# Query features of two tiles computed in 32-row by 64-column pieces of TensorE, in a fused attention and feed-forward kernel

## The chip, the cores and the metric

One core of a Trainium2 chip runs the kernel. The metric is the device time of one execution in microseconds (us). Before the change the median of three runs is 238.67 us (238.15 to 242.1).

## What is computed

Four sequences of 1088 positions with 4 heads of 32 go through a linear attention whose features are products of two small projections; the result, 4352 tokens of 128, goes through a feed-forward network with 2048 hidden units. Cut from the reference:

```
def phi(x):                                   # S1, S2: 8 x 32
    a = np.einsum('rd,bhsd->bhsr', S1, x)
    b = np.einsum('rd,bhsd->bhsr', S2, x)
    return np.einsum('bhsi,bhsj->bhsij', a, b).reshape(*x.shape[:-1], 64)
q_p, k_p = phi(q), phi(k)
kv = np.einsum('bhsf,bhsd->bhfd', k_p, v);  z = np.sum(k_p, axis=2)
num = np.einsum('bhsf,bhfd->bhsd', q_p, kv)
den = np.einsum('bhsf,bhf->bhs', q_p, z)[..., None] + 1e-06
x = (num / den) laid out as (4352, 128)
out = (s * np.maximum(x @ w_in, 0) ** 2 + b) @ w_out
```

## The kernel before

Tokens are cut into nine tiles, tile 0 of 256 columns and tiles 1 to 8 of 512 (`TILES`, L26), always with features or channels on the 128 partitions. Data types are float32; the two big matrix products of the feed-forward part are made of three products of split operands (high and low halves, `wih`, `wil`, `woh`, `wol`, `xh`, `xl`, `uh`, `ul`), all on TensorE.

The names in the code: `kvphase(b)` makes the key features of a sequence and sums them against the values into `kv` (L193). For a query tile, the two projections have to be spread from 8 + 8 rows a head to 64 products a head, which fill 128 partitions in two groups g. There are two ways to do it. Tile 0 uses `first_features` (L280): the weights `srep` already hold every projection row repeated eight times, so four products with all 128 rows give both factors in PSUM tile `hp`; ScalarE copies one factor to `br` (L291) and VectorE multiplies (L293) into `pq`. All other tiles use `qfeatures` (L336): four small products give the bare projections (L343), a copy takes them to `abq`, and SyncE's queue writes them to DRAM (`qa` twice 32 KB, `qb` four times 128 KB) and reads them back repeated (`pq` and `br`, 512 KB each, L363 and L365); VectorE multiplies (L367). `qattend(t)` then makes numerators and denominators; for tile 1 it is `direct_attend` (L371), which divides without DRAM, and for tiles 2 to 8 the denominators go by DRAM: `dc`, `num`, `rd` and four `rr` transfers (L427 to L444). `ffn(t, jp)` is a pair of 128 hidden units: products into `hp`, relu and square on ScalarE (L483, L485), a split into `uh` and `ul` (L146, L493), products into `ops`.

PSUM has two buffers each of `hp` (two banks), `ops` and `psa`. Every engine runs its instructions in program order. The program order is written out by hand: `ORDER` (L34) is a list of tokens, and each token runs one generator to its next yield. `z` is a dummy product that fills TensorE (L589); `Lk0`, `Lq1`, `Lv0`, `Lw0`, `Ls` issue loads; `k0`, `q1`, `n1`, `p`, `f`, `w0` are steps of the key phase of a sequence, features and attention of a tile, features and attention of tile 0, and the split of a block of weights; `31` is a step of the pair 1 of tile 3. `ON_DVE` (L37) says which copies VectorE makes and not ScalarE. All DMAs are issued by SyncE in this order too.

Of the kernel before, what the change touches and what calls it, by code (L numbers as in the profile page):

```python
# [24 lines left out]
NMAX = 512  # L25
# [33 lines left out]
def attn_ffn_kernel(ctx: ExitStack, tc: tile.TileContext, qT, kT, vp, s64, cst, w_in, w_out, outT):  # L59
    nc = tc.nc  # L60
    PSUM = bass.MemoryType.PSUM
    const = ctx.enter_context(tc.tile_pool(name="const", bufs=1))
    p1 = ctx.enter_context(tc.tile_pool(name="p1", bufs=1))
# [4 lines left out]
    ps_h = ctx.enter_context(tc.tile_pool(name="ps_h", bufs=2, space=PSUM))  # L68
# [6 lines left out]
    tiles = plan_tiles()  # L75
# [4 lines left out]
    qT_t, w_raw, k_in, v_in = {}, {}, {}, {}  # L80
# [176 lines left out]
    qfeat, xhl, x_first = {}, {}, []  # L257
# [8 lines left out]
        xhl[t] = (xh, xl)  # L266
        yield

    srep = const.tile([P, 2, 2, P], F32, name="srep")

    def first_weights():
        for g in range(2):
            w = sk[:, 32 * g:32 * g + 32].rearrange("p (j w i) -> p w j i", j=2, w=2)
            nc.scalar.copy(out=srep[:, 1, g].rearrange("p (j i x) -> p j i x", i=R, j=2),
                           in_=w[:, 1].unsqueeze(2).broadcast_to([P, 2, R, R]))
            nc.vector.tensor_copy(out=srep[:, 0, g].rearrange("p (j i x) -> p j i x", i=R, j=2),
                                  in_=w[:, 0].unsqueeze(3).broadcast_to([P, 2, R, R]))
        yield

    def first_features(t):  # L280
        N = tiles[t][1] - tiles[t][0]
        pq = p1.tile([P, 2, NMAX], F32, name="pq")
        br = p1.tile([P, 2, NMAX], F32, name="br")
        ab = ps_h.tile([P, 2, 512], F32, name="hp")
        for w in (1, 0):
            for g in range(2):
                nc.tensor.matmul(ab[:, w, g * N:(g + 1) * N], srep[:, w, g], qT_t[t][:, :N],
                                 start=(g == 0), stop=(g == 1), skip_group_check=True)
        yield
        ab = ab[:, :, :2 * N].rearrange("p w (a n) -> p w a n", a=2)  # L290
        nc.scalar.copy(out=br[:, :, :N], in_=ab[:, 1])  # L291
        yield
        nc.vector.tensor_tensor(out=pq[:, :, :N], in0=ab[:, 0], in1=br[:, :, :N], op=ALU.mult)  # L293
        qfeat[t] = pq
        yield
# [295 lines left out]

    with tc.manual_schedule():
        gens = {"z": keep_warm(), "Ls": load_s(), "s": s_phase(), "Lcst": load_constants(),
                "sr": first_weights(), "p": first_features(0), "f": first_attend(0)}
        for b in range(B):
            gens[f"Lk{b}"], gens[f"Lv{b}"], gens[f"k{b}"] = load_k(b), load_v(b), kvphase(b)
        for i, x in enumerate(pieces):
            gens[f"Lw{i}"], gens[f"w{i}"] = load_weights(*x), split_weights(*x)
        for t in range(NT):
            gens[f"Lq{t}"], gens[f"q{t}"], gens[f"n{t}"] = load_q(t), qfeatures(t), qattend(t)  # L600
            for jp in range(NPAIR):
                gens[f"{t}{jp}"] = ffn(t, jp) if t else first_ffn(jp)
        for c in ORDER.split():
            next(gens[c], None)
# [47 lines left out]
```

## Time and profile before

| | before |
|---|---|
| median of three runs | 238.67 us (238.15 to 242.1) |
| the profiled execution, its own time | 239.63 us |
| its span | 237.9 us |
| TensorE busy | 229.4 us |
| ScalarE busy | 189.5 us |
| VectorE busy | 176.2 us |
| DMA | 29.84 MB |

The span runs from the first to the last instruction that the profiler recorded; 1.73 us of the run's time lie around it. TensorE's matmuls are pipelined, so durations of neighbours overlap, and the pace of a group is read from the start of one row to the start of the next. An f32 matmul is listed twice (x8 for four instructions).

### The profile page before, as it was taken

The page shows a single profiled execution, that of the slowest core. Times are in us where ns is not written, and L with a number is a line of the kernel's source. Part 1 is how long each engine was busy: PE and PEld are TensorE (multiplying, and loading weights), DVE is VectorE, ACT ScalarE, POOL GpSimd, SP SyncE. Part 2 cuts the span into 40 slices and gives each one's busy share as a digit, 9 for nine tenths or more (in the row PEclk, how much of TensorE's full clock was granted, in tenths as well). Part 3 has the DMA queues.
Part 4 walks back from the last instruction along what each step waited for, and adds up shares of the span by engine and source line. Part 5 has one row for each costly group of instructions (what it writes and reads, how often), then busy time and mean ns, then how long its engine had stood idle before and what let it go on. Part 6 is the DMA issues. An engine that isn't in the chain of part 4 may idle for free.

```text
span 237.9 us, 4007 instructions
## 1 busy us (share of the span) xinstructions
PE 229.4 (96%) x1507; PEld 178.1 (75%) x1508; DVE 176.2 (74%) x236; ACT 189.5 (80%) x238; POOL 2.3 (1%) x15
## 2 busy tenths in 40 slices
PE   8898799899999999999999999999999999999994
PEld 2666568677787876888878768868888888888783
DVE  1789699799987696586965678877758657566783
ACT  3258489698699987779886999697897979897971
POOL 3000000000000000000000000000000000000000
PEclk9999999999999999999999999999999999999999
DMA  6999999578782721472044157201200201000101
GB/s 174 291 388 363 312 294 286 190 204 239 168 235 94 231 55 29 120 193 96 4 118 148 52 106 210 69 3 41 73 0 0 90 0 47 0 0 0 45 4 44
DMA packets 18332, 29.84 MB, mean 125 GB/s; under 512 B 4296, under 2 KB 10440, under 8 KB 18312
## 3 DMA queue, kind: packets, MB, share of 16 engines
q1 hardware_dynamic: 18312, 29.57, 42.1%
q8 instruction: 12, 0.20, 0.3%
q14 instruction: 8, 0.07, 0.1%
HBM read 21.59 MB, written 7.00 MB: 120 GB/s over the span
## 4 chain that ended last, share of the span: by engine, by line
PE 80%; DMA 14%; SPq 2%; ACT 1%; DVE 1%; issue 0%; DVEq 0%
PE ops L499 38%; PE hp L499 36%; DMA qt<-qT 3%; PE psa L416 3%; DMA br<-qb 3%; DMA raw<-w_in 3%; DMA vt<-vp 3%; DMA qb<-abq 2%; PE psa L343 1%; PE psa L224 1%; PE psa L499 1%; ACT w L127 1%; SPq L86 1%; PE psa L202 1%; DVE pq L367 1%
## 5 line engine op out<-in xcount | busy, mean ns | idle before, releaser
L493 DVE TENSOR_TENSOR ul<-u,uh 128x1024 fp32r<-128x1024 f32 (+1 forms) x69 | 81.3, 1183 | 10.4 <-ACT uh L146 9.2
L483 ACT ACTIVATE u<-hp 128x1024 f32<-128x1024 f32 (+1 forms) x72 | 70.2, 976 | 20.7 <-PE hp L499 10.7
L485 ACT ACTIVATE u<-u 128x1024 f32<-128x1024 f32 (+1 forms) x72 | 72.2, 1012 | 1.5
L499 PE MATMUL hp<-xh,wil 128*128 128x512 f32 (+1 forms) x140 | 54.7, 390 | 0.0
L499 PE MATMUL hp<-xl,wih 128*128 128x512 f32 (+1 forms) x140 | 53.3, 381 | 0.0
L499 PE MATMUL hp<-xh,wih 128*128 128x512 f32 (+1 forms) x140 | 53.3, 381 | 0.0
L146 DVE CAST uh<-u 128x1024 fp32r<-128x1024 f32 x45 | 30.9, 689 | 30.0 <-ACT u L485 27.7
L499 PE MATMUL ops<-uh,wol 128*128 128x512 f32 (+1 forms) x136 | 52.2, 384 | 0.0
L499 PE MATMUL ops<-ul,woh 128*128 128x512 f32 (+1 forms) x136 | 51.9, 382 | 0.0
L499 PE MATMUL ops<-uh,woh 128*128 128x512 f32 (+1 forms) x136 | 51.9, 381 | 0.0
L499 PEld LDWEIGHTS hp<-xh,wil 128*128 128x128 f32 x140 | 26.3, 188 | 9.8 <-issue 4.0
L499 PEld LDWEIGHTS ops<-uh,wol 128*128 128x128 f32 x136 | 25.5, 188 | 6.3 <-issue 1.2
L499 PEld LDWEIGHTS hp<-xh,wih 128*128 128x128 f32 x140 | 26.3, 188 | 5.1
L499 PEld LDWEIGHTS hp<-xl,wih 128*128 128x128 f32 x140 | 26.3, 188 | 4.8 <-DVE xl L265 0.2
L499 PEld LDWEIGHTS ops<-ul,woh 128*128 128x128 f32 x136 | 25.6, 188 | 5.2 <-DVE ul L493 0.2
L499 PEld LDWEIGHTS ops<-uh,woh 128*128 128x128 f32 x136 | 25.5, 188 | 4.9
L146 ACT CAST uh<-u 128x1024 fp32r<-128x1024 f32 (+1 forms) x24 | 23.0, 958 | 0.5
L367 DVE TENSOR_TENSOR pq<-pq,br 128x1024 f32<-128x1024 f32 x8 | 9.6, 1206 | 3.3 <-DMA br<-qb 3.3
L210 DVE TENSOR_TENSOR ph<-ab 128x768 f32<-128x768 f32 (+2 forms) x9 | 11.0, 1218 | 0.1
L224 PEld LDWEIGHTS psa<-ph,vt 128*33 128x33 f32 x288 | 8.2, 111 | 1.4 <-issue 1.0
L224 PE MATMUL psa<-ph,vt 128*33 128x64 f32 x288 | 8.8, 220 | 0.0
L577 ACT ACTIVATE ot<-ops,bias,cst_sb 128x512 f32<-128x512 f32 (+1 forms) x9 | 6.7, 745 | 2.7 <-PE ops L499 2.6
(91 smaller groups left out, 145.4 us busy)
## 6 DMA issues: line engine op xcount, KB each, us to landing
qb<-abq SPq DMA_DIRECT2D x32, 128.0 KB
pq<-qa SPq DMA_DIRECT2D x8, 512.0 KB
br<-qb SPq DMA_DIRECT2D x8, 512.0 KB
qt<-qT SPq DMA_DIRECT2D x8, 256.0 KB
raw<-w_in SPq DMA_DIRECT2D x4, 512.0 KB
raw<-w_out SPq DMA_DIRECT2D x4, 512.0 KB
rr<-rd SPq DMA_DIRECT2D x28, 64.0 KB
outT<-ot SPq DMA_DIRECT2D x7, 256.0 KB
```

The source lines that it names most:

```text
L86: nc.sync.dma_start(out=kt[:, c * P:(c + n) * P], in_=kT[:, b * SP + c * P:b * SP + (c + n) * P])
L127: nc.scalar.activation(out=out, in_=high.bitcast(F32), func=AF.Abs, scale=2.0 ** -112)
L146: (nc.vector.tensor_copy if key in ON_DVE else nc.scalar.copy)(out=out, in_=in_)
L210: nc.vector.tensor_tensor(out=ph[:, H * c0:H * (c0 + n)], in0=ab[:, :, 0].unsqueeze(3).broadcast_to([P, H * n, R, R]), in1=ab[:, :, 1].uns ...
L224: nc.tensor.matmul(kvp[64 * g:64 * g + VW, 64 * j:64 * j + 64], v_in[b][:, c0 + c, 2 * j + g], ph[:, H * c0 + 2 * (g * n + c) + j].rearran ...
L367: nc.vector.tensor_tensor(out=pq[:, :, :N], in0=pq[:, :, :N], in1=br[:, :, :N], op=ALU.mult)
L416: nc.tensor.matmul(ps[j][64 * g:64 * g + n, e0:e1], kv_st[b][64 * j:64 * j + 64, g, :n], pq[64 * j:64 * j + 64, g, e0:e1], start=True, sto ...
L483: nc.scalar.activation(out=u[:, :, :N], in_=hp[:, :, :N], func=AF.Relu)
L485: nc.scalar.activation(out=u[:, :, :N], in_=u[:, :, :N], func=AF.Square)
L493: nc.vector.tensor_tensor(out=ul[:, :, :N], in0=u[:, :, :N], in1=f32(uh[:, :, :N]), op=ALU.subtract)
L499: nc.tensor.matmul(out, w, x, start=(first and k == 0), stop=(last and k == len(terms) - 1), skip_group_check=True)
L577: nc.scalar.activation(out=ot[:, s], in_=o[:, :N], func=AF.Identity, scale=s_col, bias=bias)
```

## The change

`first_features` becomes `wide_features`, and tile 1 uses it too (`WIDE`). The weights `srep` now hold for each head its 32 input rows and 64 repeated columns; `s_raw` grows from 128 to 160 columns to carry them. For each factor w, pair j and group g one product takes the 32 rows of head 2j+g and writes 64 partitions (those of j) of PSUM bank g, so eight products of 256 columns do 256 tokens: one such step for tile 0, two for tile 1, each followed by a copy on ScalarE and a multiplication on VectorE. Tile 1's small products, its copy `abq`, its eight DMAs and its multiplication of 1024 columns go. `ORDER` and `ON_DVE` are new throughout.

```
-ORDER = """z z z Lq1 z z z Ls s sr s Lk0 Lcst Lk0 Lk0 Lv0 Lq0 Lw0 z z z z z z Lv0 Lv0 q1 q1 s k0 k0
+ORDER = """z z z z z z z z z z Lk0 Ls z s sr Lk0 Lq0 Lq1 Lk0 Lv0 Lv0 Lw0 Lv0 z z Lcst Lk1 s s k0 k0
...
+WIDE = (1,)
...
-    s_raw = const.tile([P, 128], I32, name="s_raw")
+    s_raw = const.tile([P, 160], I32, name="s_raw")
...
-    srep = const.tile([P, 2, 2, P], F32, name="srep")
+    srep = const.tile([P, 2, R, R], F32, name="srep")
     def first_weights():
...
+        w = sk_all[:, 64:].rearrange("p (w i) -> p w i", w=2)
+        nc.scalar.copy(out=srep[:, 1], in_=w[:, 1].unsqueeze(1).broadcast_to([P, R, R]))
+        nc.vector.tensor_copy(out=srep[:, 0], in_=w[:, 0].unsqueeze(2).broadcast_to([P, R, R]))
+        yield
+
+    def wide_features(t):
+        n = tiles[t][1] - tiles[t][0]
+        M = 256
+        if t == 0:
+            pq = const.tile([P, 2, M], F32, name="pq0")
+            br = const.tile([P, 2, M], F32, name="br0")
+        else:
+            pq = p1.tile([P, 2, NMAX], F32, name="pq")
+            br = p1.tile([P, 2, NMAX], F32, name="br")
+        for c in range(0, n, M):
+            s = slice(c, c + M)
+            ab = ps_h.tile([P, 2, 512], F32, name="hp")
+            for w in (1, 0):
+                for j in range(2):
+                    for g in range(2):
+                        r = slice(D * (2 * j + g), D * (2 * j + g) + D)
+                        nc.tensor.matmul(ab[64 * j:64 * j + 64, g, w * M:w * M + M],
+                                         srep[r, w].rearrange("p i x -> p (i x)"), qT_t[t][r, s],
+                                         start=True, stop=True, skip_group_check=True,
+                                         tile_position=(D * (2 * j + g), 64 * j))
+            yield
+            nc.scalar.copy(out=br[:, :, s], in_=ab[:, :, M:])
+            yield
+            nc.vector.tensor_tensor(out=pq[:, :, s], in0=ab[:, :, :M], in1=br[:, :, s], op=ALU.mult)
+            qfeat[t] = pq
+            yield
...
-                "sr": first_weights(), "p": first_features(0), "f": first_attend(0)}
+                "sr": first_weights(), "p": wide_features(0), "f": first_attend(0)}
...
-            gens[f"Lq{t}"], gens[f"q{t}"], gens[f"n{t}"] = load_q(t), qfeatures(t), qattend(t)
+            gens[f"Lq{t}"], gens[f"q{t}"], gens[f"n{t}"] = load_q(t), (wide_features if t in WIDE else qfeatures)(t), qattend(t)
...
-    s64 = s64.reshape(P, 64)
+    s64 = np.concatenate([s64.reshape(P, 64), np.tile(np.concatenate([S1.T, S2.T], 1), (H, 1))], 1)
```

Where the new order moves instructions is shown at three places. First TensorE's program behind the dummies at its start, before the change (L343 are tile 1's small products, L202 the key projections, L287 tile 0's wide products, L224 the products of key features and values):

```order
L343 MATMUL psa<-qt,sq 32x256 x4
L202 MATMUL psa<-kt,sk 32x96 x24
L287 MATMUL hp<-qt,srep 128x256 x4
L224 MATMUL psa<-ph,vt 33x64 x36
L589 LDWEIGHTS const-bfloat16-1.0
L589 MATMUL ops<-const-bfloat16-1.0 128x512
```

and the same place of the change (its L204, L297, L226 and L237 are the key projections, the new products, the value products and the transposition of the sums):

```order
L204 MATMUL psa<-kt,sk 32x96 x16
L297 MATMUL hp<-qt,srep 64x256 x8
L204 MATMUL psa<-kt,sk 32x96 x8
L297 MATMUL hp<-qt,srep 64x256 x8
L226 MATMUL psa<-ph,vt 33x64 x36
L297 MATMUL hp<-qt,srep 64x256 x8
L237 MATMUL psa<-cst_sb,kvt_96 128x97
L600 LDWEIGHTS const-bfloat16-1.0
L600 MATMUL ops<-const-bfloat16-1.0 128x512
L204 MATMUL psa<-kt,sk 32x160 x8
```

The key projections have become the first real work, tile 1's features lie around the value products, and one dummy stands behind the transposition where before three stood ahead of it and one behind. Ahead of these rows stand 12 dummies before and 13 after.

Second, SyncE's list of DMAs from the first block of weights on, before:

```order
L111 DMA raw_147<-w_in 128x1024
L95 DMA vt<-vp 128x396 x2
L111 DMA raw_257<-w_in 128x1024
L102 DMA qt<-qT 128x512
L354 DMA qa<-abq 32x256
L358 DMA qb<-abq 16x8x256 x2
L86 DMA kt<-kT 128x640
L86 DMA kt<-kT 128x512
L111 DMA raw_295<-w_in 128x1024
L111 DMA raw_297<-w_out 128x1024
L354 DMA qa<-abq 32x256
L358 DMA qb<-abq 16x8x256
```

and after:

```order
L112 DMA raw_148<-w_in 128x1024
L96 DMA vt<-vp 128x396
L121 DMA cst_sb<-cst 128x160
L87 DMA kt<-kT 128x640
L103 DMA qt<-qT 128x512 x2
L87 DMA kt<-kT 128x512
L112 DMA raw_311<-w_in 128x1024
L112 DMA raw_313<-w_out 128x1024
L96 DMA vt<-vp 128x660
L96 DMA vt<-vp 128x528
L87 DMA kt<-kT 128x640
L87 DMA kt<-kT 128x512
```

Tile 1's round trip (`qa`, `qb`, later `pq` and `br`) is gone, and the loads for the second and third sequence and for tiles 2 and 3 (`kt`, `vt`, `qt`) have moved up into its place.

Third, TensorE's program where tile 2's attention begins (L416 before, L427 after), before:

```order
L499 MATMUL hp<-xh,wil 128x512
L499 MATMUL hp<-xl,wih 128x512
L499 MATMUL hp<-xh,wih 128x512
L416 MATMUL psa<-pq,kv_86 64x320 x2
L416 MATMUL psa<-pq,kv_86 33x320 x2
L416 MATMUL psa<-pq,kv_88 64x192 x2
L416 MATMUL psa<-pq,kv_88 33x192 x2
```

and after:

```order
L510 MATMUL ops<-ul,woh 128x258
L510 MATMUL ops<-uh,woh 128x258
L510 MATMUL ops<-uh,wol 128x258
L510 MATMUL ops<-ul,woh 128x258
L510 MATMUL ops<-uh,woh 128x258
L427 MATMUL psa<-pq,kv_86 64x320 x2
L427 MATMUL psa<-pq,kv_86 33x320 x2
L427 MATMUL psa<-pq,kv_88 64x192 x2
L427 MATMUL psa<-pq,kv_88 33x192 x2
```

Twelve products of 258 columns (tile 0's second matrix) now stand ahead of tile 2's attention; before, they stood between it and the first feed-forward product of tile 2. All else between these two points is the same in number: 66 products of 512 columns, 12 of 256, 12 of 258 (24 before) and the same small ones. Over the whole program TensorE has 16 dummies before and 14 after.

## Rows read from the trace of the kernel before

**Rows 1.** The page's busy times, and the share of the 16 DMA engines in 40 slices (tenths).

```profile
span 237.9 us, 4007 instructions
PE 229.4 (96%) x1507; PEld 178.1 (75%) x1508; DVE 176.2 (74%) x236; ACT 189.5 (80%) x238; POOL 2.3 (1%) x15
...
DMA  6999999578782721472044157201200201000101
```

**Rows 2.** The busy time of each engine in two stretches (length, then busy us and instructions of PE, PEld, DVE, ACT and POOL, the granted clock, the DMA share and GB/s).

```profile
0.00:45.40 45.40, 40.18 (x512) 27.48 (x513) 34.05 (x61) 27.87 (x60) 2.27 (x15) 1.00 0.92 300
45.40:234.70 189.30, 189.20 (x1000) 150.65 (x996) 141.76 (x176) 161.67 (x178) 0.00 (x0) 1.00 0.31 84
```

**Rows 3.** Whom TensorE waited for up to 45.4 us (us in total, times, longest).

```profile
PE psa L343 <- DMA qt<-qT: 1.2, 1, 1.2
PE psa L202 <- DMA kt<-kT: 1.1, 2, 0.8
PE psa L416 <- DVE pq L367: 0.8, 1, 0.8
PE ops L589 <- PEq L644: 0.8, 1, 0.8
PE hp L287 <- DMA qt<-qT: 0.8, 1, 0.8
PE psa L202 <- ACT abq L146: 0.2, 1, 0.2
PE ops L589 <- issue: 0.2, 1, 0.2
PE psa L252 <- DVE pq L367: 0.2, 1, 0.2
```

**Rows 4.** TensorE's timeline at the start (start us, us, what, and in brackets the idle time before it and its releaser).

```profile
0.77 5.28 PE L589 MATMUL ops<-const-bfloat16-1.0 128*128 128x512 bf16 x12 [0.77 <-PEq L644]
5.98 0.64 PE L343 MATMUL psa<-qt,sq 128*32 128x256 f32 x8
6.43 0.51 PE L202 MATMUL psa<-kt,sk 128*32 128x96 f32 x16
7.11 0.88 PE L202 MATMUL psa<-kt,sk 128*32 128x96 f32 x32 [0.16 <-ACT abq L146]
8.74 2.00 PE L287 MATMUL hp<-qt,srep 128*128 128x256 f32 x8 [0.75 <-DMA qt<-qT]
10.67 2.21 PE L224 MATMUL psa<-ph,vt 128*33 128x64 f32 x72
13.03 0.60 PE L589 MATMUL ops<-const-bfloat16-1.0 128*128 128x512 bf16 x2 [0.16 <-issue]
```

**Rows 5.** TensorE's timeline at tile 2's attention and at tile 3's; the four products of 512 columns in the second take the array in quarters of 64 by 64.

```profile
44.38 1.08 PE L416 MATMUL psa<-pq,kv 64*64 64x320 f32 x16 [0.84 <-DVE pq L367]
...
58.02 1.08 PE L416 MATMUL psa<-pq,kv 64*64 64x512 f32 x8
59.03 0.50 PE L499 MATMUL ops<-uh,wol 128*128 128x512 f32 x1
```

**Rows 6.** The chain of work that ended last, in order of time, up to 45 us (start us, us, what).

```profile
5.45 6.00 DMA vt<-vp
...
36.11 6.81 DMA br<-qb
...
43.01 1.24 DVE pq L367
```

**Rows 7.** DMA issues of the whole program by tile (count, KB each).

```profile
qb<-abq SPq DMA_DIRECT2D x32, 128.0 KB
pq<-qa SPq DMA_DIRECT2D x8, 512.0 KB
br<-qb SPq DMA_DIRECT2D x8, 512.0 KB
...
qa<-abq SPq DMA_DIRECT2D x16, 32.0 KB
```

**Rows 8.** VectorE's timeline: tile 0's multiplication and tile 1's.

```profile
11.39 0.69 DVE L293 TENSOR_TENSOR pq<-hp,br 128x512 f32<-128x512 f32 x1 [0.43 <-ACT br L291]
...
28.81 1.23 DVE L367 TENSOR_TENSOR pq<-pq,br 128x1024 f32<-128x1024 f32 x1 [0.59 <-DMA br<-qb]
```

**Rows 9.** ScalarE's timeline: the copy of tile 1's small products and the copy of one factor of tile 0.

```profile
6.68 0.37 ACT L146 COPY abq<-psa 128x256 f32<-128x256 f32 x1 [1.60 <-PE psa L343]
...
10.77 0.59 ACT L291 COPY br<-hp 128x512 f32<-128x512 f32 x1 [3.72 <-PE hp L287]
```

**Rows 10.** VectorE's timeline: the last step of tile 2's attention.

```profile
68.31 0.69 DVE L265 TENSOR_TENSOR xl<-rr,xh 128x512 fp32r<-128x512 f32 x1
```

**Rows 11.** TensorE's timeline: two neighbouring products of 258 columns, and the first feed-forward product of tile 2 that needs that last step.

```profile
66.87 0.28 PE L499 MATMUL ops<-ul,woh 128*128 128x258 f32 x1
66.99 0.28 PE L499 MATMUL ops<-uh,woh 128*128 128x258 f32 x1
...
69.08 0.48 PE L499 MATMUL hp<-xl,wih 128*128 128x512 f32 x1
```

**Rows 12.** SyncE's timeline: the first and the last transfers of tile 2's attention.

```profile
46.13 1.31 SPq L427 DMA_DIRECT2D dc<-num  x2
...
61.88 1.44 SPq L444 DMA_DIRECT2D rr<-rd  x3
```

More of the change, by code (lines that the diff above doesn't have):

```diff
@@ new lines @@
+ORDER = """z z z z z z z z z z Lk0 Ls z s sr Lk0 Lq0 Lq1 Lk0 Lv0 Lv0 Lw0 Lv0 z z Lcst Lk1 s s k0 k0 k0 k0 k0 k0 p k0 k0 k0 q1 p q1 p q1 w0 w0 k0 k0 k0 Lq2 Lq3 Lk1 w0 w0 q1 k0 k0 k0 z k1 k0 q1 k0 w0 q1 f n1 Lw2 Lw1 Lv1 Lv1 w0 f k1 f f n1 q2 f q2 f Lk2 Lk2 Lw4 q2 Lw3 q2 Lq4 q2 k1 k1 k1 f f n1 q3 00 01 k1 w2 f w2 n1 w2 k1 k1 w1 w1 q3 00 01 00 k1 k1 n1 w1 w2 k2 w1 w2 01 w4 w4 w3 f k2 w2 k2 k2 Lv2 Lv2 q2 Lw5 q2 q2 Lw6 q2 Lq5 q2 q3 q3 Lk3 q3 Lw7 Lk3 q3 q3 q3 00 n1 01 03 02 w4 n1 k2 w4 k2 q4 k2 k2 w1 w3 03 02 03 02 03 w5 q4 w4 w4 w3 03 w3 04 05 k1 02 04 04 04 05 w5 n1 w3 n1 w3 04 10 11 03 05 10 05 k2 k2 w5 w5 k1 w5 w5 05 q2 w6 w6 10 11 11 12 04 05 n2 n2 10 10 12 12 12 n2 w1 11 11 12 w6 w6 15 q5 k3 13 w7 13 13 15 15 q5 n2 n2 q3 n2 q3 n2 10 12 11 n2 w6 n2 w6 13 13 06 15 15 06 06 q3 06 14 14 w7 13 k3 w7 14 06 14 07 15 q4 n2 Lq7 q4 n2 n3 07 07 n3 n3 w7 k3 w7 07 14 w7 07 17 16 k2 k2 k3 q7 06 07 14 16 16 17 17 Lv3 n2 q5 q5 n2 n2 n2 q4 q4 n3 q4 n3 q4 q4 q4 k3 n2 n2 n2 n3 q5 q7 n3 n3 n3 24 16 16 17 17 24 24 07 20 20 q4 24 24 16 17 23 20 20 20 22 n4 n4 23 23 23 23 k3 n4 22 20 24 21 n3 q7 q5 q5 q7 Lq8 q7 Lv3 n3 n3 07 n4 Lq6 n3 n3 q5 n4 q7 q5 n4 n3 n4 q5 q7 23 k3 k3 q6 26 21 21 22 22 k3 22 21 17 26 26 26 25 22 n4 21 k3 21 27 n3 q6 25 n4 q5 25 25 n3 26 n3 n5 25 27 27 27 n5 31 26 n5 27 31 31 25 30 30 30 34 k3 q8 27 32 q6 q6 q6 n4 n4 q7 n4 q6 n5 q6 q6 n5 n4 n5 q6 n5 n4 n4 17 q6 31 31 30 30 34 34 32 34 34 30 31 33 32 32 n5 27 35 n4 32 33 33 n5 32 34 36 35 35 33 33 35 k3 35 q6 36 q8 n4 n4 36 36 33 37 37 37 37 36 35 40 n6 42 40 37 40 40 40 42 42 n6 44 36 44 44 n6 n5 n5 n5 n5 n5 27 q7 q7 n6 n6 n6 42 42 n5 q8 q8 q8 n6 43 37 41 40 42 37 41 44 44 43 41 43 43 n6 q7 n5 n6 41 41 45 46 44 43 45 41 n7 n5 n5 47 43 45 45 46 46 45 47 n7 50 47 46 46 47 n7 50 50 52 45 50 47 50 52 52 46 53 47 54 50 53 53 n6 n6 n6 q8 q8 n6 q8 q8 n7 n7 n6 n7 n6 n7 52 52 q8 37 53 53 n7 n7 54 54 54 54 n6 51 56 52 51 51 53 55 51 51 56 56 47 55 55 q8 56 56 n6 n6 57 54 51 60 56 n8 55 55 57 57 57 n8 57 61 60 60 61 61 60 60 55 62 62 61 61 63 63 63 62 n7 47 n7 n7 n7 n7 57 64 65 60 61 62 62 63 62 n8 64 64 n8 63 n7 n8 n7 n8 n8 64 64 n8 65 65 66 63 67 64 65 65 66 n7 66 57 67 67 65 n7 70 71 66 66 66 67 67 70 70 70 n8 70 71 71 57 n8 n8 n8 n8 n8 n8 72 73 67 72 71 71 72 72 72 70 74 73 73 74 74 75 71 72 73 73 74 74 75 67 67 75 n8 75 76 n8 73 74 n8 80 75 76 76 76 76 77 75 80 80 77 77 77 80 80 77 81 76 82 81 81 82 83 77 80 81 81 84 83 82 82 82 83 84 84 85 81 83 83 86 82 84 84 85 85 77 86 86 87 83 84 85 85 86 86 85 86 87 87 77 86 87 87 87 87 87 87 87 87"""
@@ L35 @@
 SPLIT_0 = (tuple(range(2, 8)), (3,4,5,6,7))
 DIRECT = (1,)
-ON_DVE = """a7 a8 k21 k31 n21 n30 n31 n50 n51 n60 n61 n81 u10 u11 u12 u14 u15 u21 u23 u26 u27 u30 u31 u33 u34 u35 u36 u40 u41 u42 u45 u47 u50 u51 u52 u53 u55 u56 u57 u60 u62 u63 u64 u65 u66 u71 u72 u74 u75 u77 u81 u82 u83 u84 u85 u86 u87 w0 w5 w6 w7 x0 x1 x2 x3 x5 x6 x8""".split()
+WIDE = (1,)
+ON_DVE = """k21 k31 n21 n40 n51 n60 n61 n80 t1 t3 u06 u10 u11 u13 u14 u16 u17 u21 u24 u27 u31 u33 u34 u35 u36 u40 u41 u42 u44 u46 u47 u50 u51 u52 u53 u54 u55 u56 u60 u61 u62 u63 u64 u66 u67 u70 u71 u73 u74 u75 u80 u81 u82 u83 u84 u85 u86 u87 w3 w4 w5 w6 x1 x2 x3 x4 x5 x6 x8""".split()
@@ L152, in attn_ffn_kernel @@
     ident = cst_sb[:, CID:CID + P]
-    sk = const.tile([P, 64], F32, name="sk")
+    sk_all = const.tile([P, 80], F32, name="sk")
+    sk = sk_all[:, :64]
     sq = const.tile([P, 64], F32, name="sq")
@@ L160, in s_phase @@
         low, high = words(s_raw)
-        mag = const.tile([P, 64], F32, name="sc_m")
+        mag = const.tile([P, 80], F32, name="sc_m")
         magnitude(mag, high)
-        bits = const.tile([P, 64], I32, name="sc_b")
+        bits = const.tile([P, 80], I32, name="sc_b")
         low_bits(bits, low)
         join(bits, mag, bits)
-        with_sign(sk.bitcast(I32), high, bits)
+        with_sign(sk_all.bitcast(I32), high, bits)
         yield
@@ L267, in split_x @@
         yield
-    srep = const.tile([P, 2, 2, P], F32, name="srep")
+    srep = const.tile([P, 2, R, R], F32, name="srep")
     def first_weights():
[L272 to L277, printed above, removed]
-        yield
@@ L280, in first_features @@
[L280 to L295, printed above, removed]
+        w = sk_all[:, 64:].rearrange("p (w i) -> p w i", w=2)
```

1 line of the change is left out of this document (removed).

## Prediction

> **What bounds the kernel now.** The page comes first: TensorE is busy 96% of the span, ScalarE 80%, VectorE 74% [rows 1]. So I ask where TensorE is not busy, and cut the span where the DMA row of the 40 slices drops from nines [rows 1]. From 45.40 to 234.70 us TensorE idles 0.10 us in 189.30; up to 45.40 it is busy 40.18, so it idles 5.22 [rows 2]. In between nothing can be gained by earlier data, and each microsecond of TensorE's work counts. In the first 45.40 us both count: the work and the idle time. The kernel ends when that first stretch ends plus a fixed 189 us plus a tail of 3.2 us (237.9 less 234.70).
>
> Next, who causes the 5.22 us: 0.77 is the start of the program [rows 4], the other 4.45 are mostly data. Loads of queries and keys make 1.2 + 1.1 + 0.8, the wait of tile 2's attention for its multiplication 0.8 [rows 3], and that multiplication itself waits for `br`, which comes back from DRAM at 42.9 (36.11 + 6.81) [rows 6]. The 16 DMA engines are busy 0.92 of this stretch at 300 GB/s [rows 2]. So the first stretch is a queue of bytes, and TensorE is partly filled with dummies there: 12 at the start, 0.43 us apart (5.98 less 0.77, over 12), and four later at 0.3 [rows 4].
>
> **The change, part by part.**
>
> TensorE's work that goes: tile 0's four full products, 10.67 - 8.74 = 1.93 us, or 0.48 each; tile 1's four small ones, 6.43 - 5.98 = 0.45; of the dummies three later ones (0.9) less one more at the start (0.43), so 0.47 [rows 4]. Together 2.85.
>
> TensorE's work that comes: three steps of eight products, 32 rows by 64 columns of the array, 256 columns long. No row shows this form. If the four row pieces ran one after another, each product at the 0.48 of rows 4, a step would take 3.86 us; if all four ran at once and nothing else were paid, 0.96. The nearest row is tile 3's attention: four products of 512 columns in quarters of 64 by 64, 59.03 - 58.02 = 1.01 us [rows 5]. There too different input rows go into the same columns of the array, each of the four pieces streams 512 columns, as in a step here, and they do run at once, since one after another they would take four times 0.96. I take 1.01, so 3.03 for three. Nothing below 0.96 is to be had, because every row piece must stream its 512 columns. The net is 3.03 - 2.85 = +0.18 us of TensorE's work. By itself the wide form is no gain.
>
> One rule of the Trainium skill speaks against the 1.01: "TensorEngine Tiling (Array Packing)", Restrictions and Gotchas, PSUM Pressure, says that different row tiles cannot access one PSUM bank at the same time; here heads 0 and 2 (rows 0 and 64) both write bank 0 of `hp`, and heads 1 and 3 bank 1, though other partitions. The products of rows 5 write a bank of their own for each half of the rows, so no trace here tests it; by the rule at most two would run at once, which is the rival "in pairs" below.
>
> DMA: tile 1's round trip goes: 2 x 32 + 4 x 128 + 512 + 512 = 1600 KB, eight issues [rows 7]. At 300 GB/s [rows 2] that is 5.4 us of the queue. In SyncE's order all else ahead of tile 2's `br` is the same set of loads, 16 KB of `s_raw` apart, so `br` should land near 42.9 - 5.4 = 37.5, and tile 2's product be free at 37.5 + 1.24 + 0.14 = 38.9 (that multiplication and the gap behind it, 43.01 to 44.38 [rows 5, 6]). TensorE, with no wait at all, would be there at 44.38 - 4.45 + 0.18 + 1.44 = 41.6; the 1.44 are the twelve products of 258 columns that now stand ahead of it, 0.12 each (66.99 - 66.87) [rows 11]. So that wait goes with 2.7 us to spare, and the waits for `kt` and `qt` with it, since those loads stand earlier in the queue and on less traffic.
>
> ScalarE and VectorE: for tile 1 a copy of 0.37 and a multiplication of 1.23 become two copies of 0.59 and two multiplications of 0.69: +0.81 and +0.15 us [rows 8, 9]. They are busy 27.87 and 34.05 of 45.40 [rows 2], so this lies in their idle time; without that cover it would cost 0.96.
>
> What TensorE will still wait for, I follow along the new order. After 13 dummies (0.77 + 5.6 = 6.4) come three groups of key projections (0.44 each), two steps at 1.01 and two thirds of the value products (2.2 us for all) [rows 4]: it asks for the last third of sequence 0's values at 11.2. They landed at 11.45 [rows 6] and stand at much the same depth of the queue: 0.3 us. Then small products of `f`, `n1`, `q2` and `q3` follow each other through two `psa` buffers, each to be emptied by ScalarE or VectorE first; I count four such hand-overs at 0.2, as the short waits of rows 3: 0.8. Then the first feed-forward products of tile 1 need `xl`, which VectorE makes behind two blocks of weights: a guess of one such VectorE step, 0.7. Together 1.8 left of 4.45; the bounds are 0 and all 4.45.
>
> Tile 2's chain: in the trace its attention begins at 44.38 and its last step ends at 69.00 [rows 5, 10]; TensorE wants it at 69.08 and is held up a little (0.48 for a product that else takes 0.39) [rows 11]. This chain has no slack. Twelve products leave the stretch, so TensorE now comes 1.44 us sooner after the start of the chain. But SyncE's list from the first `dc` to the last `rr` of tile 2 shrinks from 25 DMAs to 18; it took 46.13 to 63.32, 0.69 each [rows 12], so about 4.8 us are there to shorten the chain. I take 0; the other bound is 1.44 and more.
>
> **The sum.** -4.45 + 1.8 + 0.18 = -2.5 us. Own time 239.63, span 237.9: the span becomes 235.4 and that run 237.1. The median of the runs shown, 238.67, lies 0.96 under the profiled run; 238.67 - 2.5 = **236.2 us**. With idle time between 0 and 3.3 left, 234.4 to 237.7.
>
> **The rivals.**
>
> - *In pairs*: two row pieces at a time, a step 1.93, +0.92 for each of three: 236.2 + 2.8 = 239.0, no change. For it: the new form puts two row pieces on one bank; against it: rows 5.
> - *One after another*: a step 3.86, +8.6 in all: 244.8, slower by over 2%. It lies in the three L297 groups, all before 15 us, and decides from about 3.4 us a step (243.4 - 236.2 over three, plus 1.01); at 1.84 a step the gain is gone. Against it: the quarters of rows 5 run at once.
> - *Tile 2 late*: the chain keeps its 24.6 us, TensorE stops 1.4 us, up to 2.5 with ScalarE's copies in SyncE's way: 237.6 to 238.7. For it: rows 10 and 11 show no slack. Against it: seven DMAs fewer.
> - *Other waits take over*: with the bytes gone, ScalarE and VectorE, which feed the small products, hold TensorE for as long as DMA did: 238.9. For it: VectorE is busy 34.05 of 45.40 [rows 2]; against it: a quarter of its time is still free.
>
> **How the numbers follow.** Forecast 0.60 (234.4 to 237.7), tile 2 late 0.14, in pairs 0.11, other waits 0.08, one after another 0.05, something better 0.02. The range 234.4 to 239.6 takes in all but the last two and the far end of the pairs. About 2% is what a measurement of this kernel can tell from no change: 233.9 and 243.4. To be faster than that, 4.77 us would have to go, and the idle time holds 4.45: 0.02. Slower: one after another, and a little for a stall in the new order that I have not seen: 0.06. Within 2%: 0.92.
>
> **What would show it.** L297 groups of 1.0 us each (right), 1.9 or 3.9 (wrong). DMA waits of TensorE up to 45 us under 0.5 in all, idle time without the start under 2.5, and `br` of tile 2 landed before TensorE asks for it. The long stretch starting 2 to 3 us earlier and still idling under 0.5. I am wrong if TensorE waits at tile 2's first feed-forward product for L267, or if new waits for VectorE or ScalarE before 40 us sum to over 3.

## The result, and the profile of the changed kernel

The changed kernel takes 241.46 us (median of 4 runs, 241.42 to 242.43), the kernel before, beside it, 238.77 us (4 runs, 238.15 to 242.1): a ratio of 1.013 [1.009, 1.017]. It is slower by 1.3%, where 236.2 us had been forecast, and lies above the range of 234.4 to 239.6. The profiled execution has 241.45 us, with a span of 239.7; before it was 239.63 and 237.9, so the two profiles show 1.8 of the 2.7 us.

The page of the changed kernel comes first, as in [rows 1]:

```profile
span 239.7 us, 4059 instructions
PE 233.4 (97%) x1537; PEld 178.6 (74%) x1538; DVE 176.7 (74%) x237; ACT 189.4 (79%) x237; POOL 2.2 (1%) x15
...
DMA  6999896088566654660264065011000110100011
```

TensorE is now idle for 239.7 - 233.4 = 6.3 us, where it was 8.5. So 2.2 us of idle time went, as hoped. But TensorE is busy for 4.0 us more, and the forecast gave it 0.18 of added work. The next view says where: the busy times of each engine in the stretch up to 45.40 us and in the one behind it (columns as in [rows 2]; the second is 191.0 us long here, and was 189.3).

```profile
0.00:45.40 45.40, 42.42 (x557) 29.55 (x559) 35.62 (x64) 30.47 (x63) 2.25 (x15) 1.00 0.83 271
45.40:236.40 191.00, 190.96 (x982) 149.00 (x980) 140.56 (x173) 158.94 (x175) 0.00 (x0) 1.00 0.31 82
```

Up to 45.40 TensorE does 557 matmuls, where it did 512, and idles 2.98 us instead of 5.22. Behind it, it takes 190.96 us for 982 matmuls, where 1000 took 189.20. So the stretch that nothing was to touch has become slower, without any idle time in it. What TensorE still waits for, in the whole span, are two rows (columns as in [rows 3]):

```profile
PE ops L510 <- DVE wol L485: 1.8, 1, 1.8
PE ops L600 <- PEq L656: 0.8, 1, 0.8
```

All waits for DMA are gone; 0.8 is the start of the program (it was there before), and one wait of 1.8 us is new. TensorE's timeline around the places of [rows 4, 5] (columns as there):

```profile
0.77 5.61 PE L600 MATMUL ops<-const-bfloat16-1.0 128*128 128x512 bf16 x13 [0.77 <-PEq L656]
6.32 0.87 PE L204 MATMUL psa<-kt,sk 128*32 128x96 f32 x32
7.11 1.09 PE L297 MATMUL hp<-qt,srep 32*64 32x256 f32 x16
8.14 0.54 PE L204 MATMUL psa<-kt,sk 128*32 128x96 f32 x16
8.60 1.09 PE L297 MATMUL hp<-qt,srep 32*64 32x256 f32 x16
9.63 2.48 PE L226 MATMUL psa<-ph,vt 128*33 128x64 f32 x72
12.04 1.09 PE L297 MATMUL hp<-qt,srep 32*64 32x256 f32 x16
13.06 0.46 PE L237 MATMUL psa<-cst_sb,kvt 97*128 97x97 f32 x2
...
41.73 0.39 PE L510 MATMUL ops<-uh,wol 128*128 128x258 f32 x1 [1.76 <-DVE wol L485]
...
43.57 1.08 PE L427 MATMUL psa<-pq,kv 64*64 64x320 f32 x16
44.58 0.50 PE L510 MATMUL hp<-xh,wil 128*128 128x512 f32 x1
```

A wide step takes 8.14 - 7.11 = 1.03, 1.03 and 1.02 us. Tile 2's attention begins at 43.57 with no wait ahead of it, 0.81 us sooner than in [rows 5], and the twelve products of 258 columns (1.44 us) lie behind TensorE by then: it is 2.25 us ahead. All of that, and 1.8 us more, is lost behind this point.

How, is seen in TensorE's timeline in the middle of the long stretch, at the first and the tenth of ten neighbouring feed-forward products of 512 columns. First the kernel before:

```profile
189.78 0.39 PE L499 MATMUL ops<-uh,woh 128*128 128x512 f32 x1
...
191.82 0.39 PE L499 MATMUL ops<-uh,woh 128*128 128x512 f32 x1
```

and the changed one:

```profile
189.66 0.40 PE L510 MATMUL hp<-xh,wih 128*128 128x512 f32 x1
...
191.75 0.39 PE L510 MATMUL ops<-uh,woh 128*128 128x512 f32 x1
```

Nine steps take 2.04 us before (0.2267 each) and 2.09 after (0.2322). Each start follows at once on the one before, nothing waits; every product is a little longer. Over all neighbouring products of 512 columns behind 100 us the mean from one start to the next, the **pace** in what follows, is 227.0 ns before and 232.7 after (some 550 of them in each; the few steps over 300 ns are left out). The kernel has 128 products in each of three `hp` groups and 126 in each of three `ops` groups, 762 in all: 762 x 5.7 ns = 4.3 us. The granted clock is 1.00 in both.

### The profile page after: what moved, and what is told of

It reads as the page before. It is cut to its first block, busy times and chain, and to the rows that moved or that the text cites. A ratio compares the mean times of both kernels' runs of the same rounds, so it can differ in the third digit from the quotient of the medians.

```text
span 239.7 us, 4059 instructions
## 1 busy us (share of the span) xinstructions
PE 233.4 (97%) x1537; PEld 178.6 (74%) x1538; DVE 176.7 (74%) x237; ACT 189.4 (79%) x237; POOL 2.2 (1%) x15
## 4 chain that ended last, share of the span: by engine, by line
PE 95%; issue 2%; DVE 1%; ACT 0%; ACTq 0%; DVEq 0%
PE hp L510 39%; PE ops L510 39%; PE psa L226 4%; PE psa L427 3%; PE ops L600 2%; PE psa L204 2%; PE psa L354 2%; PE hp L297 1%; PE psa L510 1%; PE psa L254 0%; ACT u L494 0%; PE psa L237 0%; PE hp L315 0%; PE psa L407 0%; DVE w L143 0%
## 5 line engine op out<-in xcount | busy, mean ns | idle before, releaser
L510 PE MATMUL ops<-uh,wol 128*128 128x512 f32 (+1 forms) x136 | 53.0, 389 | 1.8 <-DVE wol L485 1.8
L510 PE MATMUL hp<-xh,wih 128*128 128x512 f32 (+1 forms) x140 | 53.9, 385 | 0.0
L510 PE MATMUL hp<-xl,wih 128*128 128x512 f32 (+1 forms) x140 | 53.9, 385 | 0.0
L510 PE MATMUL ops<-uh,woh 128*128 128x512 f32 (+1 forms) x136 | 52.6, 387 | 0.0
L510 PE MATMUL ops<-ul,woh 128*128 128x512 f32 (+1 forms) x136 | 52.5, 386 | 0.0
L147 DVE CAST uh<-u 128x1024 fp32r<-128x1024 f32 (+1 forms) x48 | 32.8, 684 | 26.2 <-ACT u L496 17.3
L147 ACT CAST uh<-u 128x1024 fp32r<-128x1024 f32 (+1 forms) x21 | 20.3, 969 | 1.2 <-PE ops L510 0.7
L226 PEld LDWEIGHTS psa<-ph,vt 128*33 128x33 f32 x288 | 8.2, 111 | 1.7 <-issue 0.9
L226 PE MATMUL psa<-ph,vt 128*33 128x64 f32 x288 | 9.0, 220 | 0.1
L378 DVE TENSOR_TENSOR pq<-pq,br 128x1024 f32<-128x1024 f32 x7 | 8.5, 1211 | 0.0
```

The lines of the kernel that those rows point to most:

```text
L226: nc.tensor.matmul(kvp[64 * g:64 * g + VW, 64 * j:64 * j + 64], v_in[b][:, c0 + c, 2 * j + g], ph[:, H * c0 + 2 * (g * n + c) + j].rearran ...
L378: nc.vector.tensor_tensor(out=pq[:, :, :N], in0=pq[:, :, :N], in1=br[:, :, :N], op=ALU.mult)
L510: nc.tensor.matmul(out, w, x, start=(first and k == 0), stop=(last and k == len(terms) - 1), skip_group_check=True)
```

## The experiments

**What could slow each product.** Each product is the same instruction on the same shapes. What differs, besides the order of the work around it, is where the tiles lie in SBUF. `s_raw` grew by 128 bytes in each partition; `sk_all`, `sc_m` and `sc_b` grew from 64 to 80 columns, 256 to 320 bytes, and every tile allocated behind one of them moves by 64 bytes. The weights lie behind the first two of the four, 128 + 64 = 192 bytes further by the remainder, and the streamed tiles behind all four, 320 bytes further, or 64 by the remainder. The build's addresses, with the remainder by 256 bytes behind (`wih` stands for the four weight tiles, `xh` for the tiles streamed through TensorE, `xh`, `xl`, `uh`, `ul`, which all have one remainder):

```
          wih                xh
before    25088  (0)         124416  (0)
after     23744  (192)       135488  (64)
```

The theory was that these addresses set the pace; the rivals were that the new order or the other spread of copies over engines does. Beside that stood the 1.8 us wait. The padding below changes no work; only the columns allocated differ.

**e1_lines**, the changed kernel with the three tiles in 96 columns, 80 used, so that all behind them lies at multiples of 128 bytes again:

```diff
-    sk_all = const.tile([P, 80], F32, name="sk")
+    sk_all = const.tile([P, 96], F32, name="sk")[:, :80]
-        mag = const.tile([P, 80], F32, name="sc_m")
+        mag = const.tile([P, 96], F32, name="sc_m")[:, :80]
-        bits = const.tile([P, 80], I32, name="sc_b")
+        bits = const.tile([P, 96], I32, name="sc_b")[:, :80]
```

> The changed kernel with sk, sc_m and sc_b in 96 columns instead of 80, the same 80 used; every later tile then starts on a multiple of 128 bytes of its partition again, as in the kernel before, instead of 64 past one. Theory 'addresses': the pace of the 512-column products in the long stretch falls from 232.5 ns to 226.7, and with some 800 of them the time falls by 4.5 to 237.0 us. Rival 'packing': the 32-row pieces (or the new order) leave TensorE slower whatever the addresses: 241.5 us, pace 232.5 ns.

Measured: 237.53 us (10 runs, 237.06 to 238.88) against 239.0 (25 runs), ratio 0.994 [0.991, 0.997]; pace 227.0. The pace is back, with the new order and the new spread untouched, and the change is a small gain.

**e2_before_shift**, the kernel before with `sk` alone moved to 80 columns, 64 used, so that all behind it lies 64 bytes further:

```diff
-    sk = const.tile([P, 64], F32, name="sk")
+    sk = const.tile([P, 80], F32, name="sk")[:, :64]
```

> The kernel before with sk in 80 columns instead of 64, the same 64 used: nothing else, so every later tile starts 64 bytes past a multiple of 128. Theory 'addresses': pace 232.5 ns, time up by 4.5 to 243.2 us. Rival 'packing': 238.7 us, pace 226.7 ns.

Measured: 239.92 us (10 runs, 238.2 to 241.64), ratio 1.005 [1.001, 1.009]; pace 227.0. Tiles at 64 bytes past a multiple of 128 are not slow by themselves: that form of the theory fell. Here weights and streamed tiles moved alike, both to remainder 64.

**e3_copy_on_act**, the changed kernel with one copy, `k21`, back from VectorE to ScalarE; its sister `k20` was there already:

```diff
-ON_DVE = """k21 k31 n21
+ON_DVE = """k31 n21
...
```

> The changed kernel with the copy k21 of sequence 2 (the second half of the sums) on ScalarE instead of VectorE. Theory 'one queued wait': VectorE no longer stands 2.4 us for ScalarE's first half, wol is ready before TensorE asks, the 1.76 us wait goes: 239.8 us, pace still 232.5 ns. Rival 'data': tile 2's br lands too late to use it and a wait for the multiplication L378 takes its place: 241 us.

Measured: 238.83 us (10 runs, 238.56 to 239.12), ratio 0.999 [0.997, 1.002]; pace 232.7. The waits of TensorE in it:

```profile
PE ops L600 <- PEq L656: 0.8, 1, 0.8
PE psa L226 <- DMA vt<-vp: 0.6, 1, 0.6
PE psa L354 <- DVE rx L327: 0.2, 1, 0.2
```

The wait for `wol` is gone. What made it, VectorE's timeline of the changed kernel shows:

```profile
35.50 0.68 DVE L504 TENSOR_TENSOR ul<-u,uh 128x516 fp32r<-128x516 f32 x1
38.62 0.29 DVE L147 COPY kvt<-psa 33x128 f32<-33x128 f32 x1 [2.44 <-issue]
...
40.99 0.69 DVE L485 TENSOR_TENSOR wol<-w,woh 128x512 fp32r<-128x512 f32 x1
41.60 0.69 DVE L504 TENSOR_TENSOR ul<-u,uh 128x516 fp32r<-128x516 f32 x1
42.20 1.22 DVE L378 TENSOR_TENSOR pq<-pq,br 128x1024 f32<-128x1024 f32 x1
```

VectorE stands for 2.44 us ahead of its half of the copy `kvt`. The row's releaser is "issue", so the page names no culprit; ScalarE's timeline does:

```profile
38.27 0.26 ACT L147 COPY kvt<-psa 33x128 f32<-33x128 f32 x1
```

ScalarE's half ends at 38.53, and VectorE's begins at 38.62. In the program VectorE's half waits for the semaphore that ScalarE's half raises; both write `kvt`. ScalarE, busy without a gap, comes to it behind four other operations from 36.24 on; VectorE stands meanwhile, and the steps of the weight block `wol` queued behind it come late. With both halves on ScalarE, in e3_copy_on_act, the same step for `wol` starts at 38.03 instead of 40.99:

```profile
38.03 0.69 DVE L485 TENSOR_TENSOR wol<-w,woh 128x512 fp32r<-128x512 f32 x1
38.64 0.69 DVE L504 TENSOR_TENSOR ul<-u,uh 128x516 fp32r<-128x516 f32 x1
39.25 1.22 DVE L378 TENSOR_TENSOR pq<-pq,br 128x1024 f32<-128x1024 f32 x1
```

**e4_both**, the edits of e1_lines and e3_copy_on_act together.

> Both edits: 96 columns and k21 on ScalarE. Theories 'addresses' and 'one queued wait' together: 241.5 - 4.5 - 1.7 = 235.3 us, under both kernels. If packing slows TensorE: 239.8 us. If the wait moves to the data: 236.8 us.

Measured: 234.29 us (4 runs, 234.25 to 235.32), ratio 0.981 [0.976, 0.986]; pace 226.9. From e3_copy_on_act to this the padding gives 0.999 - 0.981 = 1.8%, or 4.3 us: what the pace had given by itself.

**Which addresses?** Four paddings with the remainder of weights and of streamed tiles moved apart. `sk_all` lies ahead of both, `sc_m` and `sc_b` between them. The theories were that the weights' address decides, that the streamed tiles' does, or how the two lie to each other.

**e5_moving**, the changed kernel with `sk_all` and `sc_b` padded and `sc_m` not (weights 0, streamed tiles 192):

```diff
-    sk_all = const.tile([P, 80], F32, name="sk")
+    sk_all = const.tile([P, 96], F32, name="sk")[:, :80]
-        bits = const.tile([P, 80], I32, name="sc_b")
+        bits = const.tile([P, 96], I32, name="sc_b")[:, :80]
```

> The changed kernel with sk and sc_b in 96 columns: the split weights start at a multiple of 256 bytes (remainder 0), the streamed tiles xh, xl, uh, ul with remainder 192. In the runs so far the pace was 226.7 ns at remainders (weights, streamed) of 0, 0 (twice) and 64, 64, and 232.5 ns at 192, 64. Theory 'same remainder' (slow whenever weights and streamed tiles differ by 256 bytes' remainder): pace 232.5 ns, 241.5 us. Theory 'weights' (slow when the weights lie at 192, where a 512-byte row of weights straddles differently): 226.7 ns, 237.5 us. Theory 'streamed' (slow only when the streamed tiles lie 64 off): 226.7 ns as well, unless 192 is as bad as 64.

**e6_weights**, the changed kernel with `sc_b` alone padded to 96 (weights 192, streamed tiles 128):

```diff
-        bits = const.tile([P, 80], I32, name="sc_b")
+        bits = const.tile([P, 96], I32, name="sc_b")[:, :80]
```

> The changed kernel with sc_b in 96 columns: weights at remainder 192 of 256 bytes, as in the changed kernel, streamed tiles at 128. 'Same remainder': 232.5 ns, 241.5 us. 'Weights': 232.5 ns, 241.5 us. 'Streamed' (a streamed tile is slow when it is not on 128 bytes): 226.7 ns, 237.5 us.

**e7_before_gap**, the kernel before with `sc_b` in 96 columns, 64 used, and nothing else touched (weights 0, streamed tiles 128):

```diff
-        bits = const.tile([P, 64], I32, name="sc_b")
+        bits = const.tile([P, 96], I32, name="sc_b")[:, :64]
```

> The kernel before with sc_b in 96 columns, 64 used: weights at remainder 0, streamed tiles at 128. 'Same remainder': pace 232.5 ns, 243.3 us. 'Weights' and 'streamed': 226.7 ns, 238.9 us.

**e8_same**, the changed kernel with `sc_b` in 112 columns (both at 192):

```diff
-        bits = const.tile([P, 80], I32, name="sc_b")
+        bits = const.tile([P, 112], I32, name="sc_b")[:, :80]
```

> The changed kernel with sc_b in 112 columns: weights and streamed tiles both at remainder 192 of 256. 'Same remainder': 226.7 ns, 237.5 us. 'Weights': 232.5 ns, 241.5 us. 'Streamed' (not on 128 bytes): 232.5 ns, but then the shifted kernel before, 64 off throughout, should not have kept 226.7.

These four are single runs (the kernel before beside them: 238.85, median of 20), so they are judged by the pace in their profiles:

| kernel | weights / streamed tiles, remainder by 256 | pace, ns | time, us |
|---|---|---|---|
| before | 0 / 0 | 227.0 | 238.77 |
| e1_lines | 0 / 0 | 227.0 | 237.53 |
| e2_before_shift | 64 / 64 | 227.0 | 239.92 |
| e8_same | 192 / 192 | 226.9 | 238.32 |
| e4_both | 0 / 0 | 226.9 | 234.29 |
| after | 192 / 64 | 232.7 | 241.46 |
| e3_copy_on_act | 192 / 64 | 232.7 | 238.83 |
| e5_moving | 0 / 192 | 233.3 | 242.16 |
| e6_weights | 192 / 128 | 233.3 | 243.12 |
| e7_before_gap | 0 / 128 | 232.5 | 244.46 |
| e10_32bytes | 0 / 32 | 233.3 | 239.4 |

The weights' address alone doesn't decide (0 is fast in e1_lines and slow in e5_moving and e7_before_gap), nor does the streamed tiles' (192 is slow in e5_moving and fast in e8_same). In all eleven the pace is fast where the two remainders are equal (three pairs tried), and slow where they differ (five pairs tried). In e8_same the streamed tiles lie 111872 bytes behind the weights, 437 times 256, so an equal remainder by 512 isn't needed; by 128 isn't enough (after: 192 and 64). One row of the kernel before with its padding, and one of the changed kernel with equal remainders, show it without any mean, in the busy times of the same 36 us (182 to 218, columns as in [rows 2]). First e7_before_gap:

```profile
182.00:218.00 36.00, 36.00 (x156) 29.20 (x155) 23.34 (x27) 31.02 (x32) 0.00 (x0) 1.00 0.06 23
```

then e8_same:

```profile
182.00:218.00 36.00, 36.00 (x161) 29.80 (x160) 24.36 (x27) 32.20 (x34) 0.00 (x0) 1.00 0.07 23
```

TensorE is never idle in either and does 156 or 161 matmuls, at the same granted clock. Before and after have 161 and 156 there: a padding has exchanged the kernels' places.

The times of three single runs hold something else besides the pace. In e6_weights, e7_before_gap and e8_same the granted clock fell to its lower level, 1.2 GHz, for a few microseconds, behind waits of TensorE of 1.74, 1.20 and 1.84 us. In e8_same the wait is the one for `wol` (first the stretch from 40 to 44 us, columns as in [rows 2], then TensorE's timeline):

```profile
40.00:44.00 4.00, 2.78 (x16) 2.56 (x20) 3.93 (x7) 2.14 (x3) 0.00 (x0) 0.68 0.00 0
...
41.22 0.42 PE L510 MATMUL ops<-uh,wol 128*128 128x258 f32 x1 [1.84 <-DVE wol L485]
...
45.38 0.50 PE L510 MATMUL hp<-xh,wil 128*128 128x512 f32 x1
```

From the first product behind the wait to the first feed-forward product behind tile 2's attention it takes 45.38 - 41.22 = 4.16 us; the changed kernel, with a wait for `wol` too but a granted clock of 1.00, takes 44.58 - 41.73 = 2.85. So some 1.3 us of the time of e8_same are the clock, and the times of these three rows cannot be compared more finely than that.

**e10_32bytes**, e4_both with `sc_b` in 104 columns: a difference of only 32 bytes.

```diff
-        bits = const.tile([P, 96], I32, name="sc_b")[:, :80]
+        bits = const.tile([P, 104], I32, name="sc_b")[:, :80]
```

> The kernel of e4_both with sc_b in 104 columns, 80 used: streamed tiles 32 bytes past the weights' remainder instead of 64 or 128. 'Same remainder' down to the byte: pace 232 to 233.5 ns, 239 us. If only whole steps of 64 bytes count: 226.7 ns, 234.4 us.

Measured: 239.4 us (one run), pace 233.3, where e4_both has 226.9. No partial price for a smaller difference.

**e9_one_buffer**, e4_both with `xh` in 544 columns, so that its second buffer alone, which tiles 1, 3, 5 and 7 use, lies at remainder 128. In the paddings above all that lies behind `sc_b` moves together; here one streamed buffer does:

```diff
-        xh = p2.tile([P, NMAX], F32R, name="xh")
+        xh = p2.tile([P, NMAX + 32], F32R, name="xh")
```

> The kernel of e4_both with xh in 544 columns, 512 used: of all streamed tiles only the second buffer of xh now differs from the weights' remainder (128 of 256 bytes), the first, xl, uh and ul keep 0. Theory 'same remainder', acting product by product: the products that stream the second buffer of xh (two of three hp products of every second tile) take 232.5 ns from start to start, the rest 226.7; some 130 products slower by 6 ns make 0.8 us: 235.1. Rival 'whole layout' (something else in the layout slows TensorE as a whole, or ScalarE and VectorE writing at other offsets): no difference between the buffers.

Measured: 236.44 us (one run), mean pace 228.2. By stretches it is 229.3, 229.7 and 229.7 where tiles 3, 5 and 7 run (100 to 110, 140 to 152, 190 to 199 us) and 226.7 where 4, 6 and 8 do. So the slow pace follows the buffer, tile by tile. Product by product it doesn't: from 190 to 200 us the products of `uh` and `wol`, both at remainder 0, have 231.0, those of `xl` and `wih` 226.7. A product's pace depends on its neighbours too; on which, these runs don't tell.

**e11_values_first**, e4_both with the last load of sequence 0's values ahead of the first block of weights, since the only DMA wait of e3_copy_on_act was for it:

```diff
...
-Lv0 Lv0 Lw0 Lv0 z z Lcst
+Lv0 Lv0 Lv0 Lw0 z z Lcst
...
```

> The kernel of e4_both with the third load of sequence 0's values issued ahead of the first block of weights. If TensorE's wait for these values (0.2 to 1.0 us in the runs so far) is 512 KB of weights in front of them, it goes and the time falls by 0.2 to 0.6 below e4_both. If ScalarE then waits for the weights instead and passes it on by the copies behind, nothing is gained: same as e4_both, 234.3 us.

**e12_both_again**, e4_both once more on the same chip, to compare.

> The kernel of e4_both once more, timed in five rounds on the chip of e11: 234.3 us, a ratio of 0.981 to the kernel before.

Measured: 235.14 us (6 runs, 234.58 to 236.24), ratio 0.984 [0.981, 0.988], and 235.02 (5 runs, 234.68 to 235.26), ratio 0.984 [0.980, 0.988]. The order of the loads gains nothing: e11_values_first has no wait for `vt` (e4_both had 0.2), but 0.3 for `rc` and 0.3 of issue; and e12_both_again, with the old order, has no wait for `vt` either. The first stretch of e12_both_again:

```profile
0.00:45.40 45.40, 44.39 (x587) 31.36 (x589) 37.97 (x66) 32.73 (x66) 2.25 (x15) 1.00 0.81 271
```

It idles 1.01 us, 0.8 of it the start. So the version with both edits beats both kernels, the one before by 1.6 to 1.9%: about 4.0 to 4.7 us, near the 4.45 us that this kernel's first stretch idled behind the start.

## Why the prediction was wrong

**The step that failed** is in the first paragraph: "The kernel ends when that first stretch ends plus a fixed 189 us plus a tail of 3.2 us". It wasn't fixed. From the start of tile 2's attention to the end it is 239.7 - 43.57 = 196.1 us, where it was 237.9 - 44.38 = 193.5, though 1.44 us of work had moved ahead of that point: 4.0 us more. 762 products at 5.7 ns more make 4.3. In e1_lines, where the padding alone differs, tile 2's attention begins at 43.88 of 236.1 us, so the rest is 192.2, which is the 193.5 - 1.44 = 192.1 of the kernel before: with equal remainders the step would have held.

```profile
43.88 1.08 PE L427 MATMUL psa<-pq,kv 64*64 64x320 f32 x16
```

The runs showed the cause as far as it was tried: four small tiles that grew, in code that the forecast read only for what it computes and loads. That the kernel before had equal remainders was no row that I had asked for, and e7_before_gap shows that one padding takes it away. None of the rivals on record was this one.

With that left aside, point by point:

- *Wide steps, 1.01 us each*: right, 1.02 to 1.03. "In pairs" and "one after another" are out. The rule of the Trainium skill weighed there ("TensorEngine Tiling (Array Packing)", PSUM Pressure) isn't borne out in this form: two row pieces wrote other partitions of one bank, and all four ran at once.
- *DMA, 5.4 us less*: right in what hangs on it. There is no wait for DMA in the changed kernel, and VectorE took `br` of tile 2 at 42.20 straight behind its `ul`. No row read here gives the landing itself, forecast for 37.5; in e3_copy_on_act VectorE took `br` at 39.25, again straight behind `ul`, so it had landed by then. Where TensorE starts sooner, the wait for the last third of the values comes back: 0.6 in e3_copy_on_act, 1.0 in e1_lines, against the 0.3 of the forecast.
- *Waits left, 1.8 us*: near in sum (2.98 - 0.77 = 2.21 us idle without the start), by luck, for it is wrong in kind: not three small ones but one of 1.76, at `wol`, by a copy split over two engines. I had read the list of copies on VectorE as balance only. This is the rival "other waits take over", with 1.76 of its 4.45 us: the run without it is 2.5 to 3.2 us faster (241.46 to 238.83, and 237.53 to 235.02 or 234.29). In the profiles of the first pair 0.89 us of that is a sooner start (below).
- *ScalarE and VectorE hidden*: right for the 0.96 us of new work; in e12_both_again, without the split copy, they are busy 32.73 and 37.97 of 45.40 us and hold up nothing.
- *Tile 2's chain, 0*: right. Its last step on VectorE in the changed kernel:

```profile
65.11 0.69 DVE L267 TENSOR_TENSOR xl<-rr,xh 128x512 fp32r<-128x512 f32 x1
```

  It ends at 65.80, 22.2 us behind the start of the attention, where it was 24.6 [rows 5, 10], and TensorE doesn't wait for it.
- *The sum up to tile 2*: -2.5 forecast, -2.25 measured.

So up to tile 2 the change does what the forecast says; as it stands, it lost some 4 us behind that point by the addresses. With the addresses alone mended it is worth 1.5 us (e1_lines, where 2.5 was forecast), with the copy mended too 4.0 to 4.7.

**What stays open**: why the remainder matters (no run looks inside the reads), why neighbours are slowed too, and what puts e2_before_shift 0.9 us over the kernel before at the same pace. The granted clock is not it: over the runs with a mean of 0.997 or more the medians are 239.66 us (5 runs) and 238.76 (18).

## What to carry to other kernels

Where TensorE is the bound, compare the pace of its products in the steady stretch between two versions, not only its idle time: a tile that grows by 64 bytes can shift every later one, and in these runs the fast pace came only with the weights and the streamed tiles at one remainder by 256 bytes, which padding the small tiles restores. When two engines each copy half of one PSUM tile, see in both timelines which is late; the other stands, with all that is queued behind it. And a forecast that calls a stretch fixed should say what it is fixed by.

## What the hardware showed unexpectedly

**Addresses.** A stream of products of 512 columns (type fp32r, listed as f32) ran at 226.7 to 227.0 ns where weights and streamed tiles had the same remainder by 256 bytes, and at 232.5 to 233.3 where the remainders differed by 32, 64 or 128. That is 2.5% of the pace, and 4.3 us of this kernel, for nothing but where a tile lies.

**The clock behind a wait.** The granted clock fell behind a wait of TensorE of 1.84 us in e8_same and stayed up behind the 1.76 us of the changed kernel, so one profile does not tell whether a wait costs more than its length; here the fall added some 1.3 us. None of the 19 runs of e3_copy_on_act, e4_both and e12_both_again, which are rid of the wait for `wol`, has a mean granted clock under 0.997; 2 of the 10 of e1_lines, which has the wait, lie at 0.993 or less.

**The start varies.** The 13 dummies at the start are alike in all versions of the changed kernel, and yet take different times. e4_both and e12_both_again are the same program; first e4_both:

```profile
0.77 4.45 PE L600 MATMUL ops<-const-bfloat16-1.0 128*128 128x512 bf16 x13 [0.77 <-PEq L656]
5.16 0.87 PE L204 MATMUL psa<-kt,sk 128*32 128x96 f32 x32
```

then e12_both_again:

```profile
0.78 5.23 PE L600 MATMUL ops<-const-bfloat16-1.0 128*128 128x512 bf16 x13 [0.78 <-PEq L656]
5.93 0.87 PE L204 MATMUL psa<-kt,sk 128*32 128x96 f32 x32
```

They start 0.43 us apart, the pace of 512 columns at 1.2 GHz, and go over to 0.22, that of 2.4 GHz, after seven of them in the one and eleven in the other; the real work begins 0.77 us sooner or later for it, which bears on any comparison of single runs (the changed kernel began at 6.32, e3_copy_on_act at 5.43). The Trainium skill ("TensorE: Matmul & The Clock Gate", What you observe) says that the moment of this change differs from run to run, and the traces agree. The column of the granted clock shows 1.00 for the first stretch of both, so at the start the clock is better read from the distance of the dummies.
